# A fused attention and MLP kernel: batch 0's keys in two row ranges, KV sums in 64-column matmuls, zero matmuls in the head, and a new task list

## The chip, the core and the metric

The kernel runs on one core of one Trainium2 chip. Its engines work side by side, each through its own queue in order: TensorE (PE; its weight loads are shown apart, as PEld), VectorE (DVE), ScalarE (ACT), GpSimd (POOL), and SyncE (SP), which issues nearly all DMA transfers here. The metric is the device time of one execution in microseconds (us); less is better. Besides each time the profiler gives a trace of one execution: when each instruction ran, what it waited for, and which clock TensorE was granted.

## What is computed

Four batches of four heads, 1088 rows, head size 32. Queries and keys are mapped to 64 features, the outer product of two sketches of 8; attention is linear in these features; the result, 4352 tokens of 128, goes through two matrices with a SiLU between them.

```python
def phi(x):
    a = np.einsum('rd,bhsd->bhsr', S1, x)
    b = np.einsum('rd,bhsd->bhsr', S2, x)
    return np.einsum('bhsi,bhsj->bhsij', a, b).reshape(*x.shape[:-1], r * r)
q_p, k_p = (phi(q), phi(k))
kv = np.einsum('bhsf,bhsd->bhfd', k_p, v)
z = np.sum(k_p, axis=2)
num = np.einsum('bhsf,bhfd->bhsd', q_p, kv)
den = np.einsum('bhsf,bhf->bhs', q_p, z)[..., None] + 1e-06
...
h = x @ w_in                          # x: 4352 x 128, w_in: 128 x 2048
g = h * (1.0 / (1.0 + np.exp(-h)))
return (g @ w_out).astype(np.float32)  # w_out: 2048 x 128
```

## The kernel before

The kernel is a list of small named tasks. The names stand in ORDER (lines 48 to 71), and each engine runs its share of them in that order; a framework puts in the waits that the data need. So ORDER alone decides who stands behind whom in a queue. A name ends in the batch, and after a point in the piece or part.

Keys of batch b: LK loads K with 34 rows of the sequence in each partition (Kx), KT transposes it in 32x32 blocks on DVE, PK projects it with the sketches on PE (fp32, into the PSUM tile `pair`), TK brings the result back with the sequence on the partitions, KP forms the 64 products for each row, and KV sums KP times V on PE into the PSUM tile `small`. LV loads V in four parts, VB casts it to bf16. ZS sums outer products of the sketches, ZT copies them, MW and WM turn them into one more column block of the query weights WQ, which yields the denominators. KM masks the KV sum, SE spreads it with two selection matmuls, KC copies it to SBUF (KV).

Batch 0 has its own form before: K comes in three loads by strips of 5 and 4 of the 9 columns in each quarter (line 181), is projected from a 64-wide weight WF in 9 matmuls of 128x64 that write `hp`, and ACT copies the result (TK0.0 and TK0.1, line 319). The other batches project with four column tiles of 32 (line 325), and DVE transposes back. KP runs on DVE in two parts for batch 0, on POOL in three for the others (KN, line 43).

Queries go in pieces (PIECES, line 42; 17 double columns of 64 rows in each batch): QT transposes, PQ projects into `pair`, then on DVE TQ transposes back, AW multiplies, RD sums, RC inverts, AQ scales, QP forms the 64 products, TN transposes (into QU); NM multiplies by KV on PE into `pair`, and XC copies the result on ACT to xT, which holds the MLP's input. One `pair` serves PK, PQ and NM, so each of them waits until the one before has been read.

The MLP goes over chunks of tokens (SIZES, line 41: 320, seven of 512, 320, 128). For each chunk, H multiplies xT by two of the sixteen column blocks of w_in into one of the two PSUM tiles `hp`, A applies SiLU on ACT into one of eight buffers G, O multiplies by w_out and sums in the PSUM tile `op`; F transposes the sum on DVE and stores it. wi and wo cast the weights, on ACT and POOL. Chunk 1 (tokens 320 to 832) ends where batch 0's second piece does; chunk 2 needs batch 0's third and batch 1's first, chunk 3 batch 1's second, chunk 4 batch 2's first.

In the head, `begin` sets masks and zeros, `table` runs one SiLU on a single column so that ACT loads its function table, SM multiplies out the sketch weights, and fillA issues nine matmuls of zeros into `op`, which nobody reads. SP issues K, Q and V of batch 0, then w_in and w_out, the rest of Q, and the loads of later batches between the stores.

## Time and profile before

| What | us |
|---|---|
| Median of 3 runs (lowest, highest) | 108.0 (107.89, 109.19) |
| The profiled execution's own time | 107.27 |
| Its span, from the first to the last instruction | 105.5 |
| Busy in the span: PE, ACT, DVE, PEld, POOL | 91.8, 78.5, 59.3, 43.0, 23.2 |

The profile gives busy time by engine, a picture of the span in 40 slices, the chain of waits that ended last, and the costliest groups of equal instructions. In a row of the timeline, the first number is the start, the second the duration; then engine, line, operation, the tile that is written, the tiles that are read, and the shape; in brackets the idle time ahead and what ended it. The ends of matmuls are modelled, so a busy PE is not a PE at its peak.

### The profile page before, as it was taken

The page shows a single profiled execution, that of the slowest core. Times are in us where ns is not written, and L with a number is a line of the kernel's source. Part 1 is how long each engine was busy: PE and PEld are TensorE (multiplying, and loading weights), DVE is VectorE, ACT ScalarE, POOL GpSimd, SP SyncE. Part 2 cuts the span into 40 slices and gives each one's busy share as a digit, 9 for nine tenths or more (in the row PEclk, how much of TensorE's full clock was granted, in tenths as well). Part 3 has the DMA queues.
Part 4 walks back from the last instruction along what each step waited for, and adds up shares of the span by engine and source line. Part 5 has one row for each costly group of instructions (what it writes and reads, how often), then busy time and mean ns, then how long its engine had stood idle before and what let it go on. Part 6 is the DMA issues. An engine that isn't in the chain of part 4 may idle for free.

```text
span 105.5 us, 2086 instructions
## 1 busy us (share of the span) xinstructions
PE 91.8 (87%) x783; PEld 43.0 (41%) x783; DVE 59.3 (56%) x110; ACT 78.5 (74%) x98; POOL 23.2 (22%) x48
## 2 busy tenths in 40 slices
...
PEclk9995555599999999999999999999999999999995
...
GB/s 53 298 202 233 372 344 294 258 117 0 0 87 286 294 200 115 259 9 0 0 28 71 105 1 100 0 0 6 40 59 0 49 50 0 66 37 48 57 62 25
DMA packets 23757, 11.15 MB, mean 106 GB/s; under 512 B 18372, under 2 KB 22596, under 8 KB 23748
## 3 DMA queue, kind: packets, MB, share of 16 engines
...
HBM read 8.79 MB, written 2.23 MB: 104 GB/s over the span
## 4 chain that ended last, share of the span: by engine, by line
PE 57%; DVE 18%; ACT 12%; DMA 4%; issue 4%; SPq 2%; DVEq 0%; ACTq 0%
PE hp L156 23%; PE op L156 20%; ACT G L463 9%; PE pair L156 9%; PE small L156 6%; DVE QP L167 4%; DMA Kx<-in_k_dram 4%; DVE TK L334 2%; DVE QU L412 2%; SPq L443 2%; DVE KT L300 2%; DVE AQ L167 1%; ACT xT L160 1%; DVE OT L486 1%; DVE TQ L392 1%
## 5 line engine op out<-in xcount | busy, mean ns | idle before, releaser
L463 ACT ACTIVATE G<-hp 128x1024 bf16<-128x1024 f32 (+1 forms) x74 | 67.0, 957 | 8.0 <-PE hp L156 7.3
L156 PE MATMUL hp<-xT,w_in_bf 128*128 128x512 bf16 (+2 forms) x160 | 42.1, 356 | 0.9 <-ACT G L463 0.4
L156 PE MATMUL op<-G,w_out_bf 128*128 128x512 bf16 (+1 forms) x144 | 37.9, 365 | 0.2 <-DVE OT L486 0.2
L156 PEld LDWEIGHTS <-w_in_bf 128*128 128x128 bf16 x160 | 13.8, 100 | 17.3 <-issue 8.1
L156 PEld LDWEIGHTS <-w_out_bf 128*128 128x128 bf16 x144 | 13.4, 99 | 15.4 <-issue 3.1
L167 POOL TENSOR_TENSOR KP<-TK 128x768 bf16<-128x768 f32 x9 | 13.4, 1522 | 15.5 <-DVE TK L334 15.5
L486 DVE STREAM_TRANSPOSE OT<-op 128x512 f32<-128x512 f32 (+1 forms) x9 | 6.0, 662 | 15.4 <-PE op L156 15.3
L392 DVE STREAM_TRANSPOSE TQ<-pair 128x512 f32<-128x512 f32 (+3 forms) x9 | 6.2, 686 | 9.1 <-PE pair L156 9.1
L167 DVE TENSOR_TENSOR QP<-AQ,TQ 128x1024 bf16<-128x1024 f32 (+3 forms) x9 | 10.8, 1195 | 0.2
L300 DVE STREAM_TRANSPOSE KT<-Kx 128x1152 f32<-128x1152 f32 (+2 forms) x5 | 5.7, 1130 | 4.6 <-DMA Kx<-in_k_dram 4.6
L156 PE MATMUL pair<-QT,WQ 64*64 64x256 f32 (+3 forms) x72 | 6.5, 438 | 1.0 <-ACT xT L160 0.5
L160 ACT ACTIVATE xT<-pair 128x512 bf16<-128x512 f32 (+3 forms) x9 | 5.2, 578 | 2.9 <-PE pair L156 2.8
L164 POOL CAST Vb<-Vx 128x1152 bf16<-128x1152 f32 x3 | 3.4, 1144 | 17.1 <-DMA Vx<-in_v_dram 17.1
L412 DVE STREAM_TRANSPOSE QU<-QP 128x512 f32<-128x512 f32 (+3 forms) x9 | 6.1, 681 | 0.3
L156 PE MATMUL pair<-QU,KV 64*64 64x256 bf16 (+3 forms) x72 | 3.8, 286 | 2.4 <-DVE QU L412 2.4
L381 DVE STREAM_TRANSPOSE QT<-Qx 128x512 f32<-128x512 f32 (+3 forms) x9 | 5.6, 640 | 0.0
L164 POOL CAST w_out_bf<-w_out_f 128x512 bf16<-128x512 f32 x4 | 2.4, 632 | 12.9 <-DMA w_out_f<-in_moe_w_out_dram 12.9
L160 ACT ACTIVATE TK<-hp 128x320 f32<-128x320 f32 (+1 forms) x2 | 0.8, 410 | 5.8 <-PE hp L156 5.8
L156 PE MATMUL op<-zeros 128*128 128x512 bf16 x9 | 3.6, 569 | 1.2 <-DVE zeros L222 1.2
L167 DVE TENSOR_TENSOR AW<-TQ 128x128 f32<-128x128 f32 (+3 forms) x9 | 4.2, 462 | 0.3
L156 PEld LDWEIGHTS <-KP 128*64 128x64 bf16 x144 | 3.1, 123 | 2.5 <-issue 1.7
L156 PEld LDWEIGHTS <-KV 64*64 64x64 bf16 x72 | 1.8, 108 | 5.8 <-issue 4.1
...
## 6 DMA issues: line engine op xcount, KB each, us to landing
...
```

What stands on the lines that cost most here:

```text
L156: nc.tensor.matmul(dst, w, x, start=start, stop=stop, tile_position=pos, **kw)
L160: nc.scalar.activation(out=out_, in_=in_, func=ACT.Copy)
L164: nc.gpsimd.tensor_copy(out=out_, in_=in_)
L167: (nc.vector if eng == "D" else nc.gpsimd).tensor_tensor(out=out_, in0=a, in1=c, op=ALU.mult)
L300: nc.vector.transpose(out=view(KT[b % 2][:, :], n0 * P, (32, 4), (P, n1 - n0), (1, 32)), in_=view(Kx[b][:, :], n0 * D, (NC * D, 4), (1, (n ...
L334: o.add(f"TK{b}.{r}", lambda r=r: nc.vector.transpose(out=view(tk[:, :], 16 * r, (32, NC), (NC * 32, 2), (1, 16)), in_=view(pair[:, :], r ...
L381: o.add(f"QT{b}.{p}", lambda n0=n0, n1=n1: nc.vector.transpose(out=qt[:, n0 * 64: n1 * 64], in_=Qx[b][:, n0 * 64: n1 * 64]))
L392: o.add(f"TQ{b}.{p}", lambda at=at, m=m: nc.vector.transpose(out=tq[:, at * 32: (at + 2 * m) * 32], in_=view(pair[:, :], 0, (CH, 2), (1, m ...
L412: o.add(f"TN{b}.{p}", lambda at=at, rn=rn: nc.vector.transpose(out=qu[:, at * 64: (at + rn) * 64].bitcast(FP32), in_=qp[:, at * 64: (at + ...
L443: nc.sync.dma_start(dst, view(t[32 * r: 32 * (r + 1), :], y0 - t0, (32, (y1 - y0) // 32), (1, 32)))
L463: nc.scalar.activation(out=view(gb[:, :], 0, (stride, per), (1, ntok)), in_=view(hb[:, :], 0, (stride, per), (1, ntok)), func=ACT.Silu)
L486: nc.vector.transpose(out=t[:, :ntok], in_=op[:, :ntok])
```

## The change

It has eight parts:

1. Batch 0's K is loaded in two row ranges (18 and 16 of the 34 rows of each partition) and goes the way of the other batches: strips in four column tiles, two at a time, into `pair`, and back by two DVE transposes. WF and its mask go, WK is made right after SM on DVE.
2. KP of batch 0 is split into two parts on DVE and four on POOL; the other batches' KP goes to POOL in nine parts of one column each.
3. The KV sum takes two heads in one matmul: 18 of 128x64 with 128-wide weights in place of 36 of 64x32. KM reads the wider sum, and its mask drops what the two heads make of each other.
4. 33 matmuls of zeros in eleven groups (fillA, fillB, f.0 to f.8) in place of nine in one.
5. Batch 0's queries go in pieces of 6, 6 and 5, before 5, 8 and 4; the chunks are 384, seven of 512, 256, 128. Chunk 1 (384 to 896) now reaches into batch 0's third piece.
6. w_in is loaded and cast in four quarters. LV0.0 is held until LK0.0 has landed.
7. `table` goes to the end of the list, ahead of the last two SiLUs; a table load now stands where ACT's functions first ask for it.
8. ORDER is a new list; all loads stand in it ahead of the first store.

```diff
-SIZES = [320, 512, 512, 512, 512, 512, 512, 512, 320, 128]
-PIECES = [[(0, 5), (5, 13), (13, 17)], [(0, 8), (8, 17)], [(0, 8), (8, 17)], [(0, 8), (8, 17)]]
+SIZES = [384, 512, 512, 512, 512, 512, 512, 512, 256, 128]
+PIECES = [[(0, 6), (6, 12), (12, 17)], [(0, 8), (8, 17)], [(0, 8), (8, 17)], [(0, 8), (8, 17)]]
...
-FILL = {'fillA': (9, 512)}
+FILL = {'fillA': (4, 512), 'fillB': (3, 512), 'f.0': (2, 512), 'f.1': (3, 512), 'f.2': (2, 512), 'f.3': (4, 512), 'f.4': (2, 512), 'f.5': (3, 512), 'f.6': (6, 512), 'f.7': (3, 512), 'f.8': (1, 512)}
+HOLDS = {'LV0.0': 'LK0.0'}
 ORDER = """
-begin LK0.0 S1 LQ0.0 LK0.1 KT0.0 QT0.0 S2 LK0.2 fillA SM WF KT0.1 table begin2 LV0.0 LV0.2 L4 PK0.0 TK0.0
...
+LK0.0 begin S1 S2 KT0.0 LK0.1 fillA f.0 SM WK WQ0 KT0.1 LQ0.0 LV0.0 LV0.1 LV0.2 LV0.3 LI.0 LI.1 LQ0.1 LI.2
+LI.3 LO.0 LO.1 LK1 LV1.0 LV1.1 LV1.2 L4 QT0.0 f.1 PK0.0 f.2 PK0.1 TK0.1 TK0.0 KP0.0 KP0.3 f.3 ZS0 ZT0 VB0
+KP0.6 KP0.5 KP0.7 f.4 MW0 WM0 f.5 PQ0.0 TQ0.0 AW0.0 RD0.0 RC0.0 KP0.8 KV0.0 KV0.3 KV0.5 KV0.6 fillB KV0.7
...
+    def load(name, make):
+        def issue():
+            landed[name] = make()
+            if name in HOLDS:
+                tc.add_manual_dep(landed[name].ins, landed[HOLDS[name]].ins.name, mybir.DependencyInfo(
+                    mybir.DependencyClass.Sync, mybir.DependencyReason.DATA), reason="order of loads")
+        o.add(name, issue)
...
+    load("LK0.0", lambda: load_rows(k, Kx, 0, 0, 2 * NC))
+    load("LK0.1", lambda: load_rows(k, Kx, 0, 2 * NC, NY))
...
+    o.add("WK", lambda: nc.vector.tensor_tensor(
+        out=view(WK[:, :], 0, (16, 2), (8, 2), (1, 8)), in0=view(sp[:, :], 0, (8, 2), (0, 2), (1, 8)),
+        in1=view(hmask[:, :], 0, (0, 2), (1, 2), (0, 8)), op=ALU.mult))
...
-                def project_k(n0=n0, n1=n1, p=p):
-                    for n in range(n0, n1):
-                        mm(hp[0][:, p * CH + (n - n0) * 64: p * CH + (n - n0 + 1) * 64],
-                           kt[:, n * P: (n + 1) * P], WF[:, :])
-                o.add(f"PK0.{p}", project_k)
-                o.add(f"TK0.{p}", lambda n0=n0, n1=n1, p=p: copy(
-                    "A", view(tk[:, :], n0 * 32, (32, n1 - n0), (NC * 32, 2), (1, 32)),
-                    hp[0][:, p * CH: p * CH + (n1 - n0) * 64]))
...
+        halves = [(0, 2), (2, 4)] if b == 0 else [(0, 4)]
+        for p, (c0, c1) in enumerate(halves):
+            at = f".{p}" if b == 0 else ""
+            o.add(f"KT{b}{at}", lambda c0=c0, c1=c1: nc.vector.transpose(
+                out=view(kt[:, :], c0 * 32, (32, c1 - c0), (P, NC), (1, 32)),
+                in_=Kx[b][:, c0 * NC * D: c1 * NC * D]))
+
+            def project_k(c0=c0, c1=c1):
+                for c in range(c0, c1):
                     for r in range(2):
                         mm(pair[32 * c: 32 * (c + 1), r * CH: r * CH + NC * 32],
                            WK[64 * r: 64 * (r + 1), :],
...
-                        for h2 in range(2):
-                            h = 2 * r + h2
-                            mm(sp[64 * h2: 64 * (h2 + 1), 64 + 32 * r: 96 + 32 * r],
-                               kp[:, (n * 4 + h) * 64: (n * 4 + h + 1) * 64],
-                               Vb[b][:, (h * NC + n) * D: (h * NC + n + 1) * D],
-                               start=(n == 0 and r == 0), stop=(n == NC - 1),
-                               pos=(0, 64 * h2), skip_group_check=True)
+                        mm(sp[:, 64 + 64 * r: 128 + 64 * r],
+                           kp[:, (n * 2 + r) * P: (n * 2 + r + 1) * P],
+                           view(Vb[b][:, :], (2 * r * NC + n) * D, (NC * D, 2), (1, D)),
+                           start=(n == 0 and r == 0), stop=(n == NC - 1), skip_group_check=True)
```

What the new list does to the queues is seen in the built programs' own rows. Three places follow; a row has the line, the operation, the tile written, the tiles read, and the size written.

ACT before, from its first instruction to the second SiLU (G is SiLU's output, TK the old copies of the projected keys, ZT, Vb, KV and xT as above):

```order
L243 ACT_TABLE_LOAD
L243 ACTIVATE warm<-warm 128x1
L160 ACTIVATE TK_81<-hp_137 128x5x2x32
L160 ACTIVATE TK_81<-hp_137 128x4x2x32
L160 ACTIVATE ZT_85<-small 128x32
L160 ACTIVATE Vb_73<-Vx_71 128x1152
L160 ACTIVATE w_in_bf<-w_in_f 128x1024
L160 ACTIVATE KV_93<-small 128x256
L160 ACTIVATE w_in_bf<-w_in_f 128x1024
L160 ACTIVATE xT<-pair 128x2x5x32
L463 ACTIVATE G_114<-hp_137 128x2x320
L463 ACTIVATE G_115<-hp_138 128x2x320
```

ACT now, from its first table load on:

```order
L171 ACT_TABLE_LOAD
L171 ACTIVATE ZT_85<-small 128x32
L171 ACTIVATE Vb_73<-Vx_71 128x1152
L171 ACTIVATE w_in_bf<-w_in_f 128x512 x2
L171 ACTIVATE KV_93<-small 128x256
L171 ACTIVATE w_in_bf<-w_in_f 128x512
L171 ACTIVATE xT<-pair 128x2x6x32
L171 ACTIVATE w_in_bf<-w_in_f 128x512
L445 ACT_TABLE_LOAD
L445 ACTIVATE G_114<-hp_135 128x2x384
L445 ACTIVATE G_115<-hp_136 128x2x384
```

The two copies of TK are gone, w_in is cast in four parts, one of which stands behind xT, and a second table load stands right ahead of the first SiLU.

DVE before, from the first TQ of batch 0 (row of TQ<-pair) to TN of the same piece (QU<-QP):

```order
L392 STREAM_TRANSPOSE TQ_97<-pair 128x320
L167 TENSOR_TENSOR AW_99<-TQ_97 128x10x8
L167 TENSOR_TENSOR KM_91<-small,pmask 128x128
L399 TENSOR_REDUCE DN_101<-AW_99 128x10
L402 RECIPROCAL DN_101<-DN_101 128x10
L167 TENSOR_TENSOR AQ_103<-TQ_97,DN_101 128x80
L167 TENSOR_TENSOR QP_105<-AQ_103,TQ_97 128x640
L412 STREAM_TRANSPOSE QU_107<-QP_105 128x320
```

DVE now, the same stretch:

```order
L374 STREAM_TRANSPOSE TQ_97<-pair 128x384
L178 TENSOR_TENSOR AW_99<-TQ_97 128x12x8
L381 TENSOR_REDUCE DN_101<-AW_99 128x12
L384 RECIPROCAL DN_101<-DN_101 128x12
L363 STREAM_TRANSPOSE QT_79<-Qx_67 128x384
L178 TENSOR_TENSOR AQ_103<-TQ_97,DN_101 128x96
L178 TENSOR_TENSOR KM_91<-small,pmask 128x128
L178 TENSOR_TENSOR QP_105<-AQ_103,TQ_97 128x768
L374 STREAM_TRANSPOSE TQ_97<-pair 128x384
L394 STREAM_TRANSPOSE QU_107<-QP_105 128x384
```

Two steps of the next piece, QT and TQ, now stand between RC and TN of piece 0, and KM has moved behind AQ.

DVE before, from TQ of batch 1's first piece on (TQ_98, AW_100, DN_102, AQ_104, QP_106 and QU_108 are batch 1's query tiles, 512 the width of its first piece and 576 of its second; KT_77 takes batch 2's keys, OT_123 is an output of the MLP):

```order
L392 STREAM_TRANSPOSE TQ_98<-pair 128x512
L167 TENSOR_TENSOR AW_100<-TQ_98 128x16x8
L399 TENSOR_REDUCE DN_102<-AW_100 128x16
L402 RECIPROCAL DN_102<-DN_102 128x16
L167 TENSOR_TENSOR AQ_104<-TQ_98,DN_102 128x128
L167 TENSOR_TENSOR QP_106<-AQ_104,TQ_98 128x1024
L167 TENSOR_TENSOR KM_92<-small,pmask 128x128
L412 STREAM_TRANSPOSE QU_108<-QP_106 128x512
L300 STREAM_TRANSPOSE KT_77<-Kx_65 128x4x9x32
L486 STREAM_TRANSPOSE OT_123<-op 128x512
L392 STREAM_TRANSPOSE TQ_98<-pair 128x576
L167 TENSOR_TENSOR AW_100<-TQ_98 128x18x8
```

DVE now, from the same TQ on (TK_81 is batch 2's):

```order
L374 STREAM_TRANSPOSE TQ_98<-pair 128x512
L306 STREAM_TRANSPOSE KT_77<-Kx_65 128x4x9x32
L178 TENSOR_TENSOR AW_100<-TQ_98 128x16x8
L381 TENSOR_REDUCE DN_102<-AW_100 128x16
L374 STREAM_TRANSPOSE TQ_98<-pair 128x576
L178 TENSOR_TENSOR KM_92<-small,pmask 128x128
L384 RECIPROCAL DN_102<-DN_102 128x16
L178 TENSOR_TENSOR AQ_104<-TQ_98,DN_102 128x128
L178 TENSOR_TENSOR AW_100<-TQ_98 128x18x8
L178 TENSOR_TENSOR QP_106<-AQ_104,TQ_98 128x1024
L319 STREAM_TRANSPOSE TK_81<-pair 128x9x2x16 x2
L394 STREAM_TRANSPOSE QU_108<-QP_106 128x512
```

KT of batch 2, TQ and AW of batch 1's second piece, and both TK of batch 2 now stand ahead of TN (QU_108) of batch 1's first piece; before, they all stood behind it.

More of the change, by code (lines that the diff above doesn't have):

```diff
@@ L46 @@
 VB_ENG = 'APPP'
-FILL = {'fillA': (9, 512)}
+FILL = {'fillA': (4, 512), 'fillB': (3, 512), 'f.0': (2, 512), 'f.1': (3, 512), 'f.2': (2, 512), 'f.3': (4, 512), 'f.4': (2, 512), 'f.5': (3, 512), 'f.6': (6, 512), 'f.7': (3, 512), 'f.8': (1, 512)}
+HOLDS = {'LV0.0': 'LK0.0'}
 ORDER = """
-begin LK0.0 S1 LQ0.0 LK0.1 KT0.0 QT0.0 S2 LK0.2 fillA SM WF KT0.1 table begin2 LV0.0 LV0.2 L4 PK0.0 TK0.0
-PK0.1 WQ0 TK0.1 LV0.1 ZS0 ZT0 KP0.0 LV0.3 MW0 WM0 PQ0.0 LI.1 LI.0 KP0.5 LQ0.1 TQ0.0 VB0 KV0.0 AW0.0 KV0.5
@@ L51 @@
-KM0 SE0 LO.1 RD0.0 RC0.0 AQ0.0 wi.1 QP0.0 TN0.0 QT0.1 KC0 NM0.0 wi.0 XC0.0 PQ0.1 LO.0 H0.0 wo.1 H0.1 A0.0
-H0.2 A0.1 wo.0 O0.0 A0.2 H0.3 WR O0.1 QT0.2 LV1.1 H0.4 TQ0.1 AW0.1 RD0.1 RC0.1 LQ1 A0.3 wo.2 A0.4 AQ0.1
-QP0.1 LV1.2 H0.5 A0.5 O0.2 O0.3 TN0.1 NM0.1 O0.4 XC0.1 LK1 KT1 wo.3 H0.6 PQ0.2 TQ0.2 AW0.2 RD0.2 LV2.3 H0.7
-RC0.2 AQ0.2 A0.6 H1.0 O0.5 QP0.2 O0.6 A0.7 LV1.0 LV1.3 H1.1 VB1 A1.0 O0.7 LV2.2 TN0.2 QT1.0 H1.2 A1.1 F0 LK2
-LQ3 NM0.2 XC0.2 H1.3 PK1 TK1.1 O1.0 O1.1 TK1.0 A1.2 A1.3 KP1.0 ZS1 ZT1 LV2.0 MW1 QT1.1 H1.4 WM1 PQ1.0 KV1.0
```

126 lines of the change are left out of this document (52 added, 74 removed).

## The prediction

> **What bounds the kernel now.** I read the page first, then busy times by stage, then the timeline of the head and of the middle, and last the groups by shape for prices. All times are us of the profiled execution, from the start of its span.
>
> ```profile
> span 105.5 us, 2086 instructions
> ...
> PEclk9995555599999999999999999999999999999995
> ...
> GB/s 53 298 202 233 372 344 294 258 117 0 0 87 286 294 200 115 259 9 0 0 28 71 105 1 100 0 0 6 40 59 0 49 50 0 66 37 48 57 62 25
> ...
> PE 57%; DVE 18%; ACT 12%; DMA 4%; issue 4%; SPq 2%; DVEq 0%; ACTq 0%
> ```
>
> The page's second part cuts the span into 40 slices of 2.64. PE's granted clock stands at half (5) in slices 3 to 7, in the head; the DMA row holds 286 GB/s on average over slices 1 to 7. The chain of waits gives PE 57%, DVE 18%, ACT 12%. These shares average stages with different limits, so the stages come next (us; busy PE, PEld, DVE, ACT, POOL with counts; clock; DMA share; GB/s).
>
> ```profile
> 24.60:38.80 14.20, 13.20 (x145) 5.56 (x147) 11.60 (x23) 9.88 (x14) 5.38 (x5) 1.00 0.59 157
> 38.80:48.50 9.70, 8.64 (x80) 3.06 (x76) 7.34 (x12) 7.51 (x10) 1.96 (x2) 1.00 0.44 110
> 48.50:101.30 52.80, 51.36 (x410) 23.60 (x406) 24.67 (x45) 49.42 (x58) 9.11 (x7) 1.00 0.21 37
> ```
>
> After 48.5, PE is busy 51.4 of 52.8: PE is the bound there, with ACT close behind (49.4). From 24.6 to 48.5 ACT is busy 17.4 of 23.9 and DVE 18.9, so neither PE nor ACT is the whole bound: the attention of the next batch, a long chain through DVE, is late. Before 24.6 the kernel is a pure latency chain. The timeline shows its stations (start, duration, engine, line, operation, out<-in).
>
> ```profile
> 3.84 0.85 DVE L300 STREAM_TRANSPOSE KT<-Kx 128x640 f32<-128x640 f32 x1 [1.73 <-DMA Kx<-in_k_dram]
> 5.61 1.33 PE L156 MATMUL hp<-WF,KT 128*128 128x64 f32 x10 [0.32 <-DVE WF L264]
> 7.46 1.94 PE L156 MATMUL hp<-WF,KT 128*128 128x64 f32 x8 [0.53 <-ACT TK L160]
> 9.43 0.38 ACT L160 ACTIVATE TK<-hp 128x256 f32<-128x256 f32 x1 [2.03 <-PE hp L156]
> 11.30 0.81 PE L156 MATMUL pair<-QT,WQ 64*64 64x160 f32 x8 [0.38 <-DVE WQ L167]
> 12.29 0.51 DVE L392 STREAM_TRANSPOSE TQ<-pair 128x320 f32<-128x320 f32 x1
> 12.84 0.24 DVE L167 TENSOR_TENSOR AW<-TQ 128x80 f32<-128x80 f32 x1
> 15.16 0.51 DVE L412 STREAM_TRANSPOSE QU<-QP 128x320 f32<-128x320 f32 x1
> 16.25 0.44 ACT L160 ACTIVATE xT<-pair 128x320 bf16<-128x320 f32 x1 [0.87 <-PE pair L156]
> 17.81 1.25 PE L156 MATMUL hp<-xT,w_in_bf 128*128 128x320 bf16 x4
> 18.56 1.30 ACT L463 ACTIVATE G<-hp 128x640 bf16<-128x640 f32 x2 [1.87 <-PE hp L156]
> ...
> 24.63 0.59 PE L156 MATMUL hp<-xT,w_in_bf 128*128 128x512 bf16 x2
> ...
> 38.80 1.02 ACT L463 ACTIVATE G<-hp 128x1024 bf16<-128x1024 f32 x1 [0.74 <-PE hp L156]
> 45.29 1.38 DVE L300 STREAM_TRANSPOSE KT<-Kx 128x1152 f32<-128x1152 f32 x1 [1.47 <-DMA Kx<-in_k_dram]
> 46.59 0.81 DVE L334 STREAM_TRANSPOSE TK<-pair 128x288 f32<-128x288 f32 x2
> 48.46 1.94 ACT L463 ACTIVATE G<-hp 128x1024 bf16<-128x1024 f32 x2 [0.40 <-PE hp L156]
> ```
>
> The first SiLU starts at 18.56, chunk 1's first matmul (H1.0) at 24.63, chunk 2's first SiLU (A2.0) at 38.80, chunk 3's (A3.0) at 48.46. The 10 projection passes of 5.61 take 0.13 each, the 8 of 7.46 take 0.24: the clock fell in between.
>
> **The change, part by part.** The prices, by group of equal shape (busy us, mean ns) or as single pieces of the timeline, and two pieces of the chain in order of time (start, us, what):
>
> ```profile
> L167 DVE TENSOR_TENSOR QP<-AQ,TQ 128x1024 bf16<-128x1024 f32 x4 | 5.2, 1290 | 0.1
> L300 DVE STREAM_TRANSPOSE KT<-Kx 128x1152 f32<-128x1152 f32 x3 | 4.1, 1364 | 2.1 <-DMA Kx<-in_k_dram 2.1
> L392 DVE STREAM_TRANSPOSE TQ<-pair 128x512 f32<-128x512 f32 x4 | 2.9, 718 | 4.1 <-PE pair L156 4.1
> L243 ACT ACT_TABLE_LOAD x1 | 1.3, 1283 | 1.7 <-PEq L511 1.7
> L160 ACT ACTIVATE w_in_bf<-w_in_f 128x1024 bf16<-128x1024 f32 x2 | 2.1, 1052 | 0.1
> L463 ACT ACTIVATE G<-hp 128x640 bf16<-128x640 f32 x16 | 10.8, 702 | 2.8 <-PE hp L156 2.6
> L167 POOL TENSOR_TENSOR KP<-TK 128x768 bf16<-128x768 f32 x9 | 13.4, 1522 | 15.5 <-DVE TK L334 15.5
> L246 POOL CAST SEL<-ident 128x256 bf16<-128x256 f32 x1 | 0.4, 401 | 0.1
> ...
> 1.18 3.55 PE L156 MATMUL op<-zeros 128*128 128x512 bf16 x9 [1.18 <-DVE zeros L222]
> 28.21 0.72 PE L156 MATMUL pair<-KT,WK 64*32 64x288 f32 x16
> 50.54 1.63 DVE L167 TENSOR_TENSOR AW<-TQ 128x128 f32<-128x128 f32 x1
> 51.95 0.74 PE L156 MATMUL small<-Vb,KP 128*64 128x32 bf16 x36
> 58.84 3.77 ACT L463 ACTIVATE G<-hp 128x1024 bf16<-128x1024 f32 x4 [0.20 <-PE hp L156]
> 69.86 0.33 DVE L167 TENSOR_TENSOR AW<-TQ 128x128 f32<-128x128 f32 x1
> 101.25 0.29 DVE L481 COPY OT<-op 128x128 f32<-128x128 f32 x1 [1.73 <-PE op L156]
> ...
> 59.61 0.43 PE op L156 x2
> 97.98 0.46 PE hp L156 x8
> ```
>
> Keys in row ranges, projected in strips, turned on DVE (the head up to PQ0.0). LK0.0 is issued first, as before, and I keep 3.8 for its landing. The hold makes SP wait for it there, and the V pieces, w_in, w_out and K1 queue behind that wait. K1 then has 4.33 MB ahead of and with it; at 286 GB/s from 2.6 on it is in by 17.8, and DVE asks for it at 19.7, so the hold is hidden; V and the w_in quarters are earlier in the same line. On DVE: KT0.0 is 576 wide, 0.85x576/640 = 0.78 (to 4.6); WK and WQ0 are products smaller than that of 12.84, 0.4 together; KT0.1 0.78; L4 and QT0.0 0.8 (to 6.6); TK twice, 0.81 + 0.1 (to 7.5). The old ACT copy of TK ended at 9.8. The sketches have six zero matmuls ahead of them now and had nine, and PE's two halves of the projection take half of the 16 passes of 28.21 each (0.36), beside L4 and QT0.0: hidden. KP0.0 and KP0.3 have 1280 elements at 1.29 per 1024: 1.6 (to 9.1). ZS0, ZT0, MW0 run beside them. WM0 0.2 (9.3); PQ0.0 0.81x192/160, halved for a full clock, and 0.1 to arrive: done at 9.9, against 12.1.
>
> Piece 0 has six columns for five. From the start of TQ0.0 to the end of TN0.0 (QU) the old kernel took 12.29 to 15.67, 3.4; six columns give 3.8. The new list puts QT0.1 (0.55) and TQ0.1 (0.6) inside: 4.95, to 14.9. KM0, in that row too, needs KV0.8, and that needs POOL's four products (from 7.5, at most 0.6 each by the price below) and Vb (ACT, from 8): there by 12, hidden. NM0.0 takes 0.45 and XC0.0 0.5: xT is there at 15.85, against 16.69.
>
> The table. The old kernel loads ACT's table after 1.7 in idle time. The new one loads one before its first Copy, hidden, and a second right before the first SiLU, behind one more quarter of w_in: 0.53 + 1.28 after XC0.0, where H0.0 alone would ask for 0.5. First SiLU at 17.65, -0.9 on 18.56; 1.3 is lost on the table and the quarter.
> [...]
>
> To chunk 1, which now reaches into batch 0's piece 2. From TN0.0 on DVE has one unbroken queue: piece 1 (3.3 without its TQ), TQ0.2 to AQ0.2 (1.6), KT1 1.36, QP0.2 0.8, TK1 twice 0.9, TN0.2 0.5, and 0.45 of gaps (0.04 each, as between 12.29 and 12.84): to 23.85. NM0.2 and XC0.2 0.9: H1 at 24.8, as before (24.63). What is won here is 64 tokens that lie behind it already.
>
> To chunk 2. Sixteen DVE instructions from 23.85 to the end of TN1.0, among them both QT1, KT2, both TQ1, QP1.0 (1.29) and both TK2: 9.5 by their shapes, 0.6 of gaps, 0.3 of waits for POOL: 34.2. NM1.0, XC1.0 and H2.0 1.6: A2.0 at 35.8, -3.0. POOL's nine products of 256 each are bounded by the cast of 256 (0.40) and the product of 768 (1.52); I take a third of the latter and a fixed part, 0.6, since the kind is the same. They end at 23.3 + 5.4 = 28.7, and DVE asks for KM1 at 30: hidden. The row of 50.54 shows a risk that this split lowers: a DVE product that takes 0.33 at 69.86 took 1.63, until POOL's product of 1.5 had ended. With 256 at most 0.6 is lost in this way each time.
>
> To chunk 3. Twelve DVE instructions to the end of TN1.1 (7.5, 0.4 of gaps, 0.6 for POOL): 42.7. XC1.1 ends at 43.8; A2.6, KC2 and A2.7 follow: A3.0 at 46.2, -2.3. The wait of 45.29 for a K load goes, because every load now stands ahead of the stores on SP; the first stores wait there for the last loads instead, and their tile is wanted again two chunks later: hidden.
>
> From chunk 3 to the end PE's work counts. The old kernel took 52.8 from 48.46 to the last copy at 101.25. Less: 64 tokens (an eighth of 32 matmuls of 512 at 0.215 by 59.61, 0.9); PQ2.0, KV2, PK3 and ZS3, which are done earlier (0.65 + 0.7 + 0.65 + 0.3 = 2.3). More: two output pairs that are not done yet (0.9). The last chunks have 4 SiLUs of 1024 (0.94 apart at 58.84) for 8 of 640 (0.70): at most 1.8 less, and I take 0.5, as ACT bounds only a part of the tail. The sum KV3 is now 18 matmuls of 64 columns with weights of 128: the eight of 97.98 have such weights and 128 columns and take 0.058 each, so 18 take at most 1.0; the lower end is below the old 0.74, half of it, as half as many are issued. I take 1.0, +0.3. Sum -2.5.
> [...]
>
> Zero matmuls: 33 of 512 columns, 0.215 each at full clock (7.1), 0.39 by the nine that start at 1.18 and run before the clock is up (13). At full clock each group lies beside a DVE or ACT step named above and costs nothing; at half they outlast that cover and stand in PE's queue ahead of PK0, MW0 and PQ0.0. The warm activation before A9.0 adds 0.2 on ACT, beside H9.1.
>
> The sum: -2.3 - 2.5 = -4.8 on 107.27, the profiled execution (span 105.5 and 1.77 around it): 102.5. The median of the runs shown is 108.0, so the profiled one lies 0.7 low.
>
> **The rivals.** One: the clock stays half in the head in spite of the fills. For it, slice 3 fell to half not long after the nine fills had ended at 4.73; against it, fills now come every two steps. Price: the 14 fills of f.1 to f.5 at 0.18 more each, and 0.5 for the passes: 3.0 at PQ0.0, all handed on: 105.5.
>
> Two: the gain is taken off the path and nothing comes of it. PE is busy 21.8 of 23.9 from 24.6 to 48.5; if that is real work, what runs earlier only pushes other matmuls back. Then the 64 tokens (0.9) and the last chunks (0.5) remain: 105.9. Against it, PE's pieces include waits inside a group, and ACT has 6.5 idle there.
>
> Three: a table switch behind running work costs more than the load. By the rows it may cost once more the load at most, 1.3, and the whole DVE queue after XC0.1 moves with it: 103.8. No row decides it. [...]
>
> Four, slower: POOL's small products are dear. At 1.52 for 256, the upper bound, KP1 ends at 37.0 and KM1 slips by 7.2; KP2 ends at 55, KP3 at 69, and XC2.0 comes when chunk 4 has waited for it: 102.5 + 7.2 + 1 = 110.7. It decides from about 1.3 each, where the gain of 4.8 is used up. For it, no row has this shape; against it, the cast at 0.40.
>
> **How the numbers follow.** Forecast 102.5, chance 0.58; its own range is 98.5 (none of the waits for POOL 0.9, nothing lost on the table 1.3, the last chunks' 1.8 in full 1.3, KV3 at its lower end 0.6) to 104.5 (KV dearer by 0.3 in the three earlier batches too, the 1.0 of DVE gaps after 24 doubled). Rival one 0.12, two 0.13, three 0.09, four 0.08. A range that leaves out no more than 2 in 10 is 98.5 to 107, with rivals one to three in it and a table loss on top of one. Two per cent of 108.0, about what a measurement of this kernel can tell from no change, puts the borders at 105.8 and 110.2. Faster: the forecast, rival three and parts of one and two, 0.77; same 0.15; slower 0.08.
>
> **What would show it.** The granted clock without a 5 between slices 3 and 7; TK turned by 7.5 to 8; the first SiLU at 17 to 18.5, right behind a table load; H1 near 24.8; A2.0 before 37 and A3.0 before 47; POOL's products at 0.5 to 0.7; the 18 matmuls of a KV sum within 1.0. The forecast is wrong if DVE's queue from 15 to 43 runs longer than its shapes, if PE's fills outlast their cover, or if the time from A3.0 to the end stays at 52.

## The result and the profile after

The changed kernel takes 101.4 us (median of 4 runs, 101.3 to 101.7) beside 108.59 (4 runs) of the kernel before: ratio 0.936, interval 0.928 to 0.944. The profiled execution took 101.3, with a span of 99.5. The forecast was 102.5. Single times of one kernel lie up to 4.3 apart on one chip, so the readings below go by stations inside a profile, and by medians only where these are far apart.

The page of the changed kernel: span, granted clock in 40 slices, the chain of waits by engine; behind it the window that begins after PE's last pause of the head, and that of chunk 2 (from:to, length; busy PE, PEld, DVE, ACT, POOL with counts; clock; DMA share; GB/s).

```profile
span 99.5 us, 1987 instructions
...
PEclk9999999999999999999999999999999999999997
...
PE 79%; DVE 7%; ACT 4%; DMA 3%; issue 2%; ACTq 1%; DVEq 0%
```

```profile
22.70:95.60 72.90, 71.70 (x589) 34.42 (x596) 41.43 (x75) 67.73 (x83) 20.50 (x30) 1.00 0.34 68
39.75:48.30 8.55, 8.44 (x99) 4.14 (x100) 6.86 (x13) 8.55 (x12) 8.55 (x13) 1.00 0.19 34
```

The 5 is gone from the clock, PE has 79% of the chain for 57%, and from 22.7 to the last copy PE is busy 71.7 of 72.9. The chain runs through PE there, 26 us sooner than where I had seen PE become the bound. ACT is close behind (67.7 of 72.9), and in chunk 2, the second row, it runs without a pause (8.55 of 8.55) beside PE's 8.44: both are full there. The stations in the timeline of the same kernel (start, duration, engine, line, operation, out<-in, shape, count, idle time ahead and what ended it):

```profile
4.15 0.57 PE L167 MATMUL small<-ident,S 16*128 16x16 f32 x2 [0.22 <-DMA S<-in_S_dram]
5.11 1.46 PE L167 MATMUL op<-zeros 128*128 128x512 bf16 x3
6.50 1.19 PE L167 MATMUL pair<-KT,WK 64*32 64x288 f32 x8
9.83 0.85 DVE L319 STREAM_TRANSPOSE TK<-pair 128x288 f32<-128x288 f32 x2 [2.91 <-PE pair L167]
18.52 0.49 ACT L171 ACTIVATE xT<-pair 128x384 bf16<-128x384 f32 x1 [1.21 <-PE pair L167]
19.55 1.28 ACT L445 ACT_TABLE_LOAD   x1
20.84 1.51 ACT L445 ACTIVATE G<-hp 128x768 bf16<-128x768 f32 x2
21.70 0.49 PE L167 MATMUL hp<-xT,w_in_bf 128*128 128x384 bf16 x2 [1.07 <-ACT G L445]
...
39.75 5.63 ACT L445 ACTIVATE G<-hp 128x1024 bf16<-128x1024 f32 x6 [1.42 <-PE hp L167]
47.16 1.95 ACT L445 ACTIVATE G<-hp 128x1024 bf16<-128x1024 f32 x2
...
95.60 0.29 DVE L463 COPY OT<-op 128x128 f32<-128x128 f32 x1 [1.79 <-PE op L167]
```

The head is later than before, not earlier: TK is turned by 10.7 where 7.5 was forecast, and the first SiLU starts at 20.84 (18.56 before, 17.65 forecast). All of the gain comes behind it. The chain of waits of the same kernel shows what stands in the way (start, us, what):

```profile
5.18 1.39 PE op L167 x3
6.57 1.11 PE pair L167 x8
7.68 0.97 PE op L167 x2
8.65 1.16 PE pair L167 x8
```

These are f.1, the first half of the keys' projection, f.2 and the second half, one behind the other: 4.63 in all. The row of 47.16 is A2.7 and A3.0, so A3.0 starts at 48.09.

One station of the prediction was misnamed: the row of before at 48.46 holds two SiLUs, of which the first is A2.7 (the list puts it behind ZT2, which stands at 47.87). A3.0 of the kernel before starts at 49.38, and 51.87, not 52.8, lies between it and the last copy. By these stations, with the profiles of all the kernels below (SiLUs counted in the trace, each with its own start: A1 is the ninth, A2.0 the 17th, A3.0 the 25th; "clock up" is the first rise of PE's granted clock that the trace records):

| kernel | clock up | first SiLU | A1 | A2.0 | A3.0 | last copy | A1 to A2.0 | A2.0 to A3.0 | A3.0 to last copy |
|---|---|---|---|---|---|---|---|---|---|
| before | 4.12 | 18.56 | 25.36 | 38.80 | 49.38 | 101.25 | 13.44 | 10.58 | 51.87 |
| changed | 9.70 | 20.84 | 29.24 | 39.75 | 48.09 | 95.60 | 10.51 | 8.33 | 47.51 |
| e1 table early | 10.35 | 19.71 | 28.36 | 38.88 | 47.20 | 94.71 | 10.52 | 8.31 | 47.51 |
| e2 no fills | 4.09 | 18.07 | 27.45 | 37.96 | 46.28 | 93.79 | 10.52 | 8.31 | 47.51 |
| e3 no f.1, f.2 | 8.54 | 18.43 | 26.83 | 37.35 | 45.68 | 93.19 | 10.52 | 8.33 | 47.51 |
| e5 changed, again | 4.51 | 18.22 | 26.62 | 37.13 | 46.04 | 93.55 | 10.51 | 8.91 | 47.51 |
| e6 POOL 768 | 4.28 | 18.20 | 26.60 | 37.47 | 46.67 | 94.28 | 10.87 | 9.20 | 47.62 |
| e9 best | 9.18 | 17.61 | 26.13 | 36.64 | 44.96 | 92.47 | 10.51 | 8.32 | 47.51 |
| e10 best, dense | 4.92 | 16.98 | 25.86 | 36.38 | 45.56 | 93.08 | 10.52 | 9.19 | 47.51 |
| e11 no hold | 9.13 | 20.60 | 29.01 | 39.52 | 47.83 | 95.35 | 10.52 | 8.31 | 47.51 |
| e4 before, KV alone | 23.99 | 20.56 | 27.47 | 40.70 | 51.29 | 102.91 | 13.23 | 10.59 | 51.61 |
| e7 before, sizes | 5.54 | 19.07 | 26.73 | 40.00 | 51.01 | 102.59 | 13.27 | 11.01 | 51.58 |
| e8 before, loads first | 4.61 | 18.57 | 25.37 | 39.87 | 49.86 | 101.76 | 14.49 | 9.99 | 51.90 |
| e12 before, sizes and tail | 4.54 | 19.15 | 26.65 | 39.91 | 50.56 | 101.20 | 13.26 | 10.65 | 50.64 |

Between before and changed the last copy moves by -5.65: head +2.28, chunk 0 +1.61, chunk 1 -2.93, chunk 2 -2.25, the rest -4.36. Chunk 0 is longer, and chunk 1 shorter, in part because three pieces of PE's work have moved from behind A1 to ahead of it: batch 1's projection PK1, its sums ZS1, and NM0.2. PK1 stood at 28.21 before; NM0.2 of the kernel before, then the three in the changed kernel, whose A1 starts at 29.24:

```profile
27.42 0.31 PE L156 MATMUL pair<-QU,KV 64*64 64x128 bf16 x8 [0.40 <-DVE QU L412]
```

```profile
25.50 0.72 PE L167 MATMUL pair<-KT,WK 64*32 64x288 f32 x16
27.29 0.38 PE L167 MATMUL small<-TK 128*32 128x32 f32 x18
27.68 0.34 PE L167 MATMUL pair<-QU,KV 64*64 64x160 bf16 x8
```

So chunks 0 to 2 are best read as one: from the first SiLU to A3.0 it is 27.25 for 30.82.

### The profile page after: what moved, and what is told of

The parts are those of the page before. It is cut to its first block, busy times and chain, and to the rows that moved or that the text cites. A ratio compares the mean times of both kernels' runs of the same rounds, so it can differ in the third digit from the quotient of the medians.

```text
span 99.5 us, 1987 instructions
## 1 busy us (share of the span) xinstructions
PE 90.1 (91%) x722; PEld 41.5 (42%) x733; DVE 56.5 (57%) x111; ACT 76.4 (77%) x95; POOL 30.8 (31%) x69
## 4 chain that ended last, share of the span: by engine, by line
PE 79%; DVE 7%; ACT 4%; DMA 3%; issue 2%; ACTq 1%; DVEq 0%
PE op L167 33%; PE hp L167 30%; PE pair L167 12%; PE small L167 5%; DMA S<-in_S_dram 3%; ACT G L445 2%; ACT L445 1%; DVE KP L178 1%; DVE QP L178 1%; DVE TQ L374 1%; DVE TK L319 1%; ACTq L182 1%; ACT w_in_bf L171 1%; ACT xT L171 0%; DVE QU L394 0%
## 5 line engine op out<-in xcount | busy, mean ns | idle before, releaser
L167 PE MATMUL hp<-xT,w_in_bf 128*128 128x512 bf16 (+3 forms) x153 | 39.0, 346 | 1.2 <-ACT G L445 1.1
L167 PE MATMUL op<-G,w_out_bf 128*128 128x512 bf16 (+2 forms) x142 | 36.8, 361 | 0.3
L178 POOL TENSOR_TENSOR KP<-TK 128x256 bf16<-128x256 f32 x31 | 20.7, 704 | 13.8 <-DVE TK L319 11.2
L468 DVE STREAM_TRANSPOSE OT<-op 128x512 f32<-128x512 f32 (+2 forms) x9 | 6.0, 667 | 19.8 <-PE op L167 19.8
L167 PE MATMUL op<-zeros 128*128 128x512 bf16 x31 | 10.9, 468 | 1.4 <-DVE zeros L225 1.2
L178 DVE TENSOR_TENSOR QP<-AQ,TQ 128x1024 bf16<-128x1024 f32 (+3 forms) x9 | 11.2, 1245 | 0.2
L306 DVE STREAM_TRANSPOSE KT<-Kx 128x1152 f32<-128x1152 f32 (+1 forms) x5 | 5.6, 1123 | 1.8 <-DMA Kx<-in_k_dram 1.8
L319 DVE STREAM_TRANSPOSE TK<-pair 128x288 f32<-128x288 f32 x8 | 3.4, 460 | 4.8 <-PE pair L167 4.8
L167 PEld LDWEIGHTS <-KP 128*128 128x128 bf16 x72 | 3.7, 98 | 2.9 <-issue 0.3
L167 PE MATMUL pair<-KT,WK 64*32 64x288 f32 x64 | 4.5, 482 | 0.0
L167 PE MATMUL small<-Vb,KP 128*128 128x64 bf16 x72 | 4.1, 193 | 0.1
```

Source lines behind the costliest of these rows:

```text
L167: nc.tensor.matmul(dst, w, x, start=start, stop=stop, tile_position=pos, **kw)
L178: (nc.vector if eng == "D" else nc.gpsimd).tensor_tensor(out=out_, in0=a, in1=c, op=ALU.mult)
L306: o.add(f"KT{b}{at}", lambda c0=c0, c1=c1: nc.vector.transpose(out=view(kt[:, :], c0 * 32, (32, c1 - c0), (P, NC), (1, 32)), in_=Kx[b][:, ...
L319: o.add(f"TK{b}.{r}", lambda r=r: nc.vector.transpose(out=view(tk[:, :], 16 * r, (32, NC), (NC * 32, 2), (1, 16)), in_=view(pair[:, :], r ...
L468: nc.vector.transpose(out=t[:, :ntok], in_=op[:, :ntok])
```

## The experiments

The theory that these stations suggest: PE is the bound from the first SiLU on, so chunks 1 and later take a fixed time, and whatever the head loses or gains shows whole at the end. The rival: DVE's queue sets the pace to chunk 3, as the prediction said, and the head has slack against it.

**e1, the table load at the front.**

```diff
-LK0.0 begin S1 S2 KT0.0 LK0.1 ...
+LK0.0 begin S1 S2 table KT0.0 LK0.1 ...
-H9.1 table A9.0 A9.1 F8 O9.0 O9.1 F9
+H9.1 A9.0 A9.1 F8 O9.0 O9.1 F9
```

> The changed kernel with its table load moved from the first SiLU back to the front, as before the change; the warm activation ahead of A9.0 goes with it. Theory (PE is full from the first SiLU to the end, so what the head loses is lost for good): the first SiLU moves from 20.84 to 19.6, A3.0 from 48.1 to 47.0, the time from 101.4 to 100.3. Rival (from 22 to 36 DVE's queue for batch 1 sets the pace, and the head has slack): first SiLU 19.6, A3.0 still 48.1, time 101.4. A third way: behind the early load a load is still found at the first SiLU, and nothing moves.

Median 99.66 (97.20 to 100.42). The timeline, with no load between the quarter of w_in and the SiLU:

```profile
18.65 0.49 ACT L171 ACTIVATE xT<-pair 128x384 bf16<-128x384 f32 x1 [1.21 <-PE pair L167]
19.04 0.62 ACT L171 ACTIVATE w_in_bf<-w_in_f 128x512 bf16<-128x512 f32 x1
19.71 3.62 ACT L445 ACTIVATE G<-hp 128x768 bf16<-128x768 f32 x5
```

From the start of XC0.0 to the SiLU 1.06 for 2.32: the late load costs 1.26, just its own duration. The last copy is 0.89 earlier though TQ0.0 began 0.13 later (13.60 for 13.47). The theory holds; the head has no slack. Rival three of the prediction (a switch behind running work costs more than the load) falls: 1.28 is all there is, with 0.02 between the end of the w_in copy and the load.

**e2, no zero matmuls behind the sketches; e3, only f.1 and f.2 out.**

```diff
-FILL = {'fillA': (4, 512), 'fillB': (3, 512), 'f.0': (2, 512), 'f.1': (3, 512), 'f.2': (2, 512), 'f.3': (4, 512), 'f.4': (2, 512), 'f.5': (3, 512), 'f.6': (6, 512), 'f.7': (3, 512), 'f.8': (1, 512)}
+FILL = {'fillA': (4, 512), 'fillB': (0, 512), 'f.0': (2, 512), 'f.1': (0, 512), 'f.2': (0, 512), 'f.3': (0, 512), 'f.4': (0, 512), 'f.5': (0, 512), 'f.6': (0, 512), 'f.7': (0, 512), 'f.8': (0, 512)}
```

> The changed kernel without the zero matmuls after the sketches (f.1 to f.8 and fillB at a count of 0; the six ahead of the sketches stay). Theory (they hold the clock and pay for it, though f.1 and f.2 stand on the chain of waits with 2.4): the granted clock falls to half somewhere in slices 3 to 8; TK is turned 1.8 earlier, but PQ0 to H0 take some 2 to 3 more and chunk 0 1.3 more; first SiLU 20 to 22, time 101.5 to 103.5. Rival (they do nothing but stand in the way): clock 9 throughout, first SiLU at 18.5 to 19, time 99.

In e3 only `'f.1'` and `'f.2'` are `(0, 512)`.

> The changed kernel without f.1 and f.2 alone (five zero matmuls ahead of PK0.0 and PK0.1, 2.5 on the chain of waits). Theory (they delay the projection and the later fills hold the clock without them): TK turned by 8.9 for 10.68, first SiLU 1.5 earlier, time 100 to 100.5. Rival (PE's full rate is won by these five, and comes later without them): the projection's passes and f.3 at half rate to about 11, TK at 10, first SiLU as it was or later, time 101 to 102.5.

e2: median 100.96, ratio 0.942 (0.936 to 0.949). e3: 98.99, 0.919 (0.909 to 0.929). The clock row of e2's page, and the keys' projection and the first SiLU in e3's timeline:

```profile
PEclk9995555569999999999999999999999999999996
```

```profile
5.75 1.97 PE L167 MATMUL pair<-KT,WK 64*32 64x288 f32 x16 [0.36 <-DVE WK L265]
18.43 3.62 ACT L445 ACTIVATE G<-hp 128x768 bf16<-128x768 f32 x5
```

Without fills the clock does fall to half, in slices 3 to 7, as the theory said, and chunk 0 takes 9.38 for 8.40. The time lies between what the theory and its rival gave. It is under the first measure of the changed kernel (101.4) and over its second (99.93, e5 below), so the medians do not tell what all the fills together are worth. Nor is the early first SiLU, 18.07, won by leaving them out: PE's granted clock rises at 4.09 in this profile, and only at 9.70 in that of the changed kernel. The profile of the changed kernel in which the rate rises as early (e5, 4.51) has its first SiLU at 18.22 and A1 at 26.62, where e2 has A1 at 27.45: beside that one, the fills win 0.83 by A1.

The later fills are worth their place: e2, which has none of them, is 1.97 behind e3 in the medians and 0.6 in the stations, though the rate rises later in e3. f.1 and f.2 are not, where the rate rises late. Without them the projection begins 0.75 earlier and is not cut in two, and 2.41 is won at the first SiLU and kept to the last copy, more than the 1.5 expected; how much of it is the rise itself (8.54 for 9.70) no run tells. The clock held without them (1.00 granted in every stretch of e3's first 96), so the rival falls.

**e4, the KV edit alone, in the kernel before.**

```diff
-                        for h2 in range(2):
...
-                               pos=(0, 64 * h2), skip_group_check=True)
+                        mm(sp[:, 64 + 64 * r: 128 + 64 * r],
+                           kp[:, (n * 2 + r) * P: (n * 2 + r + 1) * P],
...
```

> The kernel before with the KV edit alone: 18 matmuls of 64 columns for 36 of 32 in each batch. Theory (0.057 each, 4.1 for all against 3.7): nothing that can be measured, 108.2 to 109.0 beside 108.6. [...] Rival that half as many are half as dear: 1.8 less, 106.8.

Median 107.83 beside 108.14: ratio 0.999 (0.994 to 1.004). The edit costs and wins nothing. 72 passes in four sums took 4.1 in the changed kernel (144 took 3.7 before):

```profile
L167 PE MATMUL small<-Vb,KP 128*128 128x64 bf16 x72 | 4.1, 193 | 0.1
```

That is 0.057 each, by groups whose ends are modelled: the 58 ns taken in the prediction.

**e5, the changed kernel again; e6, POOL's products as before the change.**

```diff
-... KN for batches 1 to 3: ('P', 0, 1), ('P', 1, 2), ... ('P', 8, 9)
+... ('P', 0, 3), ('P', 3, 6), ('P', 6, 9)
```

> The changed kernel again, unaltered, beside the three that follow, so that they have their own measure: 101 to 102, first SiLU 20.8, A3.0 48.1, from A3.0 to the last copy 47.5.

> The changed kernel with POOL's nine products of 256 for batches 1 to 3 in three of 768, as before the change, at the same places in the list. Theory (the small products let DVE's own instructions in between and cost POOL 0.6 each, 5.4 for a batch against 4.5): the middle from A1.1 to A3.0, 18.9 now, grows by 0.5 to 1.5, the time to 102 to 103. Rival (the number of pieces does not matter for DVE, and POOL is free a little earlier): middle 18.9 within 0.2, time as the control's. From A3.0 to the end nothing changes in either, 47.5.

e5: median 99.93 (98.87 to 101.07), and its profile is 2.6 earlier at the first SiLU than that of the same kernel above. From e5's timeline:

```profile
1.19 2.74 PE L167 MATMUL op<-zeros 128*128 128x512 bf16 x6 [1.19 <-DVE zeros L225]
4.90 0.82 PE L167 MATMUL op<-zeros 128*128 128x512 bf16 x3
5.66 0.69 PE L167 MATMUL pair<-KT,WK 64*32 64x288 f32 x8
7.57 0.85 DVE L319 STREAM_TRANSPOSE TK<-pair 128x288 f32<-128x288 f32 x2 [0.85 <-PE pair L167]
18.22 3.62 ACT L445 ACTIVATE G<-hp 128x768 bf16<-128x768 f32 x5
```

The expectation of 20.8 missed. The six first fills take the same 2.74, but f.1's three take 0.82 where they took 1.46, and the first half of the projection 0.69 for 1.19: PE is at full rate from 4.51 here, and from 9.70 in the other execution. TK is turned by 8.4 here and by 10.7 there. So the 2.41 of e3 is what f.1 and f.2 cost where the rate rises late; by the medians, e3 lies 0.9 under e5 and 2.4 under the first measure of the changed kernel. Where it rises early they cost less: e10 below is without them, and its sketches begin 0.80 later than e5's (5.06 for 4.26), yet the sums ZS0 start at the same time (8.48 and 8.47), so the two groups cost about 0.8 there.

e6: median 101.62, ratio 0.929 (0.914 to 0.943), last copy 0.73 behind e5's, with 0.36 in chunk 1, 0.29 in chunk 2 and 0.11 after them. DVE's group of QP with 1152 elements in the middle, of e5 and then of e6 (busy us, mean ns):

```profile
L178 DVE TENSOR_TENSOR QP<-AQ,TQ 128x1152 bf16<-128x1152 f32 x1 | 1.7, 1665 | 0.0
```

```profile
L175 DVE TENSOR_TENSOR QP<-AQ,TQ 128x1152 bf16<-128x1152 f32 x1 | 2.6, 2574 | 0.0
```

One DVE product takes 2.57 beside POOL's product of 768 and 1.67 beside those of 256: in e6 it begins at 40.04, 0.15 behind a product of POOL that ends at 41.40, and ends itself 1.21 behind that. Beside e5 the split is worth 0.7 in the stations. But e5's chunk 2 holds a wait for a load of Q that e6's does not:

```profile
37.55 0.71 DVE L363 STREAM_TRANSPOSE QT<-Qx 128x512 f32<-128x512 f32 x1 [0.98 <-DMA Qx<-in_q_dram]
```

Beside the 8.33 of the changed kernel's first profile, which has no such wait, chunk 2 is 0.87 longer in e6. So the middle grows by 0.65 to 1.23, in the range that the theory gave; the medians lie 1.7 apart.

**e7, the chunk sizes alone in the kernel before; e12, the same with the end of the list as in the changed kernel.**

```diff
-SIZES = [320, 512, ..., 512, 320, 128]
+SIZES = [384, 512, ..., 512, 256, 128]
+e12, from H8.0 on: H8.0 A8.0 O7.5 H8.1 O7.6 O7.7 H8.2 F7 A8.1 H8.3 O8.0 O8.1 A8.2 H9.0 A8.3 O8.2 O8.3 H9.1 ...
```

> The kernel before with the chunk sizes alone: 384 first and 256 last but one, for 320 and 320, and batch 0's pieces of 6, 8 and 3 columns for 5, 8 and 4. Theory (PE's passes of 320 in the last chunks wait for eight SiLUs of 640, and 64 tokens lie ahead of A3.0): from A3.0 to the last copy 51.8 becomes 49.7, the first SiLU comes 0.4 later, and 106.5 to 107 stands beside 108.1 to 108.6. Rival (the tail's gain comes from attention done earlier, not from the sizes): tail 51 to 51.8, time 108 to 109.

> The kernel before with the chunk sizes of e7 and, from H8.0 on, the order of the changed kernel's list (H8.3 and H9.0 earlier, outputs later). Theory (the new sizes pay only with the end of the list rewritten, since H9 and the outputs waited for SiLUs there): from the copy of chunk 6 to the last, 12.8 before and 12.5 with the sizes alone, becomes 12.1 as in the changed kernel. Rival (the sizes alone gave all there is): 12.5.

e7: median 108.37, ratio 1.003 (0.999 to 1.007), and only 0.29 less from A3.0 to the last copy; its rival came true. e12: 108.27 (2 runs), and 1.23 less there. From the copy of chunk 6 to the last it is 12.79 before, 12.50 in e7, 11.56 in e12 (12.1 expected). A1 comes later in both (by 1.37 and 1.29, chunk 0 having more tokens), so the times show no gain. PE's last group in e7 waits 1.0 for a SiLU, and in before 0.6:

```profile
L155 PE MATMUL op<-w_out_bf,G 128*128 128x128 bf16 x16 | 1.2, 221 | 1.0 <-ACT G L462 1.0
```

So the sizes pay only with the end of the list written for them, and then 1.2 of the 4.36 of that stretch. The end of the list without the sizes was not run.

**e8, the late loads ahead of the first store, in the kernel before.**

```diff
-... A1.1 F0 LK2 LQ3 ...
+... A1.1 LK2 LQ3 LV2.0 LV2.1 LQ2 LV3.2 LV3.0 LK3 LV3.3 LV3.1 F0 ...
```

> The kernel before with the loads of batches 2 and 3 that stood behind stores in SP's queue (K2, K3, Q2, Q3 and six V pieces) moved ahead of the first store. Theory (batch 1 to 3 wait for a K load at 45.29, 1.47 of DVE idle): that wait goes, A3.0 comes 1 to 1.5 earlier, time 107. Rival (PE and DVE have the rest of that time to do anyway, or the loads crowd the ones that batch 1 waits for): A3.0 within 0.4 or later, time 108 to 109.

Median 109.31, ratio 1.010 (1.003 to 1.017): no gain, as the rival said. That it is a loss is not shown: seven of its ten executions had a mean granted clock of about 0.99, against seven of the nineteen of the kernel before beside them, and among these the two kernels took 109.30 to 109.67 and 109.00 to 109.73 (the last section tells what this clock means). The wait for K goes, and nothing is won by it:

```profile
35.01 2.05 DVE L166 TENSOR_TENSOR QP<-AQ,TQ 128x1024 bf16<-128x1024 f32 x1
44.81 1.33 DVE L299 STREAM_TRANSPOSE KT<-Kx 128x1152 f32<-128x1152 f32 x1
47.03 0.85 DVE L333 STREAM_TRANSPOSE TK<-pair 128x288 f32<-128x288 f32 x2 [0.89 <-ACT G L462]
```

KT3 now starts without a wait, but TK2 waits 0.89 for the path through ACT, and QP1.0 took 2.05 with POOL's cast of V beside it until 35.98; before it took 1.22 from 34.77, and that cast began at 38.69, behind it. Chunk 2 is 0.59 shorter, chunk 1 1.06 longer. The theory on this wait falls: it stood beside other waits, and to take it away alone earns nothing.

**e9, both head edits together; e10, with three more zero matmuls ahead of the sketches; e11, the changed kernel without the hold.**

```diff
 e9: e1's and e3's edits
+e10: e9's, and 'fillA': (7, 512)
-HOLDS = {'LV0.0': 'LK0.0'}
+e11: HOLDS = {}
```

> The changed kernel without f.1 and f.2 and with the table load at the front (the edits of two runs above together). Theory (whatever the head gains reaches the end whole, since the stretch from A1 on is PE's): both gains add, first SiLU at 17.0 to 17.4, from A1 to A2 10.5 and from A3.0 to the last copy 47.5 as before, time 97 to 98 beside 99 and 99.7 for each alone. Rival (batch 1's keys or the loads become the limit once the head is shorter): A1 to A2 grows to 11.5 or more and the time stays at 98.5 to 99.5.

> The one above with seven zero matmuls for four in fillA, so that PE has no pause before the sketches. [...] Rival (the rise does not depend on the pause): times spread over 2 as before, and the median is 0.5 to 1 longer than the one above.

> The changed kernel without the hold on the first V load: SP's queue does not wait for LK0.0 to land. Theory (hidden either way): K1 and Q1 land earlier by 1 to 2, nothing else moves by more than 0.3, time as the unaltered one, 99 to 101. Rival (the hold keeps V and w_in out of the way of LK0.1, Q0.0 and the sketches' loads): the sketches or KT0.1 wait 0.5 to 1.5 longer, and the time is 100.5 to 102.

e9: median 98.31 (97.22 to 98.70), ratio 0.908 (0.897 to 0.918), the lowest median, 0.3 above what was expected; its interval overlaps that of e3. Its chunk 1 takes 10.51 and its tail 47.51 like the others: the head's gains are kept. e10: 98.97, 0.916 (0.909 to 0.924), 0.66 over e9, where its rival (the rise of PE's granted clock does not depend on the pause) gave 0.5 to 1; an estimate of mine of 96.5 to 98 missed, and the intervals of the two overlap. In its profile the granted clock rises at 4.92, for 9.18 in e9. Three single times lie between 98.15 and 99.16; the fourth is 102.47, and it left no trace that would tell why. So closing the pause is not shown to make the executions equal. It is also not better, because a load is the next limit (DVE's queue in e9 and in e10):

```profile
36.62 0.71 DVE L363 STREAM_TRANSPOSE QT<-Qx 128x512 f32<-128x512 f32 x1 [0.67 <-DMA Qx<-in_q_dram]
```

```profile
37.38 0.71 DVE L363 STREAM_TRANSPOSE QT<-Qx 128x512 f32<-128x512 f32 x1 [1.74 <-DMA Qx<-in_q_dram]
```

With a shorter head DVE waits for a load of Q that was in time behind the longer one: 0.67 in e9, which chunk 2 still hides (8.32), 0.98 in e5 (8.91), and 1.74 in e10, where chunk 2 takes 9.19. The head is not all of it: this load lands at 34.42 in e3 and at 37.52 in e5, whose A1 lie only 0.21 apart. e11: 101.17, 0.940 (0.933 to 0.948); its sketches begin at 4.17 and KT0.0 at 3.62, as with the hold, and its last copy 0.25 earlier. The hold is hidden behind this head. Without it the same load of Q lands at 36.08 for 37.43, so where DVE waits for that load the hold may cost something; no run tried it there. Against e5's times it lies higher, but its profile has the first SiLU at 20.60, as late as the changed kernel's first profile, and the stations of these two agree within 0.26; so the distance from e5 is no reading of the hold.

## Why the prediction came out right

The forecast of 102.5 met 101.4 and the sign was right, but two errors stood against each other: the profile is 3.95 later at A2.0 than forecast, and then 4.85 faster from A2.0 to the last copy (2.07 to A3.0, 2.79 behind it). That the two nearly cancel is luck, and it hangs on the execution: with PE's rate up early (e5) the same kernel's profile took 99.25, 3.25 under the forecast. Step by step:

- **The head was forecast 3.2 too early** (first SiLU 17.65, measured 20.84). The step that failed: each group of zero matmuls "lies beside a DVE or ACT step named above and costs nothing". f.1 and f.2 had no such step beside them. They stand on the chain ahead of the projection, and the projection's "two halves" do not take 0.36 each: the eight passes with half the strips take 0.69 at full rate (e5), about what sixteen with all strips took in the row of 28.21, and 1.19 at half rate. TK was done 3.2 later than forecast, and the first SiLU is 3.2 later too: the steps between took their forecast time. Of the 3.2, 2.6 come with the late rise of PE's rate: in e5 the first SiLU is at 18.22, 0.6 late. The table with its quarter of w_in was priced at 1.3; without the table 1.26 is won (e1), and the quarter lies beside H0.0.
- **Rival one was set up on the wrong sign.** The clock row has no 5, so by the row that I named as the test it failed, yet its substance, PE at half rate in the head with fills standing ahead of PK0, is what this execution shows until 9.70. It put 3.0 on this; 2.6 lies between the two executions at the first SiLU. The sign should have been the duration of the passes.
- **H1 was forecast at 24.8** and its first matmul (H1.1 in the new list) is at 28.55: the head's delay, and 0.5 more.
- **From H1 to A2.0** 11.0 was forecast; 11.2 was measured (14.17 before). The number is right and the reason is not: DVE's queue was named. In e9 DVE is idle for 0.85 of chunk 1 and ACT for 1.87, PE is busy throughout, and the chunk takes 10.51 as elsewhere, so PE's own order fills that time:

```profile
26.13:36.64 10.51, 10.51 (x112) 4.47 (x108) 9.66 (x20) 8.64 (x11) 7.97 (x13) 1.00 0.77 194
```

From the end of TN0.2 (27.63) to the end of TN1.0 (36.80) DVE took 9.17, where 10.35 was forecast. From there "NM1.0, XC1.0 and H2.0" were given 1.6, and A2.0 comes 2.95 behind, since six outputs stand ahead of H2.0 in PE's queue:

```profile
36.13 0.67 DVE L394 STREAM_TRANSPOSE QU<-QP 128x512 f32<-128x512 f32 x1
37.76 1.47 PE L167 MATMUL op<-G,w_out_bf 128*128 128x512 bf16 x6
39.06 1.03 PE L167 MATMUL hp<-xT,w_in_bf 128*128 128x512 bf16 x4
```

- **From A2.0 to A3.0** 10.4 was forecast, 8.33 measured. The sum over DVE was near: the twelve instructions behind TN1.0 were given 8.5, and TN1.1 (44.06, 0.78 long) ends 8.04 behind it. What failed is the place of A2.0, which PE's queue put 1.35 later behind TN1.0 than forecast, so that DVE was that much further when chunk 2 began. In chunk 2 PE and ACT are both full; which of them sets its length no run tells.
- **From A3.0 on** -2.5 was forecast, -4.36 measured from the right station. The 64 tokens and the last chunks (0.9 and 0.5) measure 1.2 together (e12). What is done earlier was sized at 2.3 and came to more: from A3.0 to the copy of chunk 4 the changed kernel takes 20.49 for 24.15, with as many recorded matmuls of the two layers in it (79 and 79). PK3, ZS3, KV2 and one selection take 1.9 of this by the pieces of before's chain (0.73, 0.38, 0.69, 0.11), the end of PQ2.0 0.3. The rest would be the refill behind each such piece (a pair takes 0.54 there, 0.43 otherwise) and two pauses of PE (0.5); that split is read from rows and no run shows it. The kept-back pairs, put at 0.9, may be the 0.63 that the copy of chunk 7 comes later behind that of chunk 6 (6.73 for 6.10).
- **KV**: 1.0 was taken for a sum; 4.1 for four. Right, and e4 shows that the time does not move.
- **POOL**: 0.6 for a product of 256. In batch 1 nine took 5.36, 0.60 each; the four of batch 0, beside DVE's own products, took 3.52, 0.88 each (timeline of the changed kernel below): the two beside DVE's products take 1.32 and 1.07, the two behind them 0.62 each. Rival four is out, and that the split lowers the wait at DVE is shown (e6).

```profile
10.84 3.52 POOL L178 TENSOR_TENSOR KP<-TK 128x256 bf16<-128x256 f32 x4 [7.75 <-DVE TK L319]
...
27.32 5.36 POOL L178 TENSOR_TENSOR KP<-TK 128x256 bf16<-128x256 f32 x9 [3.48 <-DVE TK L319]
```

- **The loads**: that the wait of 45.29 goes was right, and it was worth nothing by itself (e8). The hold was hidden behind the late head (e11).
- **Rival two** (nothing comes of it) is out. The middle, chunks 1 and 2, shrank by 5.18; some of that is work that moved ahead of A1, and chunk 0 grew by 1.61. From the first SiLU to A3.0, which holds both, 3.57 is won though batch 3's keys came into it (PK3, ZS3) and chunk 0 has 64 tokens more, so PE's time there had not all been work.

What no run tells is which rows of the new list earn the middle's 5.18 beyond the 0.65 to 1.23 of e6 and the work that moved into chunk 0: e4, e7 and e8 leave its two chunks at 13.23 to 14.49 and 9.99 to 11.01, so neither the KV form, the sizes nor the loads alone do it, and the order itself was not taken apart.
